# Linear attention and a gated MLP on one core: a bias preset in PSUM, decays on k, DMA transposes for seven steps, natural token order, a new order of all engines

## The chip, the core and the metric

The kernel runs on one core of a Trainium2 chip. The core has five engines that run side by side, each with its own in-order list of instructions: TensorE (PE), which multiplies matrices and transposes; VectorE (DVE); ScalarE (ACT); GpSimd (POOL); and SyncE (SP), which here only issues transfers. PE's weight loads are shown as an engine of their own, PEld. Transfers run on 16 DMA engines. They are issued from queues: SP's, ACT's, and POOL's, whose transfers also convert f32 to bf16 here. PE writes its sums into PSUM, which has eight banks of 512 f32 for each of 128 partitions; everything else lies in SBUF. The metric is the device time in microseconds; less is better.

## What is computed

Two layers in a row, for 4 sequences (batches) of 768 tokens. The first is an attention with a decay per head (8 heads of 64), in blocks of 64 tokens with a running state; the second is a gated MLP that mixes tokens by the matrix W_spatial:

```python
for b in range(nb):
    intra = np.einsum('bhic,bhjc->bhij', qb, kb) * Dmask[None]
    intra = np.einsum('bhij,bhjd->bhid', intra, vb)
    inter = np.einsum('bhid,bhde->bhie', qb * lam_pow[None], kv_state)
    out[:, :, sl] = intra + inter
    kb_dec = kb * rev_pow[None]
    kv_state = lam_block[None, :, None, None] * kv_state + np.einsum('bhsd,bhse->bhde', kb_dec, vb)
...
h = np.maximum(x @ w_in, 0.0)
u, v = (h[..., :d_ff // 2].copy(), h[..., d_ff // 2:].copy())
v_n = (v - mu) / np.sqrt(var + 1e-06)
v_s = np.einsum('ts,bsd->btd', w_spatial, v_n) + b_spatial[None, :, None]
gated = u * v_s
return (gated @ w_out).astype(np.float32)
```

The inputs q, k, v are f32, 4 x 8 x 768 x 64; w_in is 512 x 1024, w_spatial 768 x 768, w_out 512 x 512. lam, one per head, lies between 0.97 and 0.99.

## The kernel before

Each batch is cut into three steps of 256 tokens, so there are 12 steps, 0 to 11; batch 0 is steps 0 to 2. A partition holds two tokens in a row (m = 0, 1), so that a load reads 512 bytes at a time. The decay between two tokens is split into a factor of the query's position (`lq`, or its inverse form `lqn`) and one of the key's (`lv`), so the mask itself (`m01`) is only zeros and ones. In the kernel before, the key's factor is multiplied into v.

The order of all work is written out by hand in `ORDER` (lines 16 to 77). A token names an operation, its indices and, last, its engine: T is PE, D DVE, A ACT, P POOL, S SP. Each engine performs its tokens in this order, and waits where an input isn't there or a buffer isn't free; nothing overtakes. The operations of a step n are:

- LK, LQ, LV (line 184): loads of k, q, v, 512 KB each, from SP, into one of three buffers each.
- KC, QC (267): casts to bf16 into `kc`, `qc`, heads side by side in pairs. VD (292): v times the key's decay, into `vd`.
- TK, TQ (300): eight transposes on PE for each of k and q; EK, EQ (310, 313) take them out of PSUM, EQ times the query's decay. For steps 8 to 11 instead QM (277) multiplies q by the decay on the way to `qc`, and DK, DQ (283, 287) transpose by DMA, from SP's queue.
- SC (329): scores, in two halves; MK (333): the mask, from PSUM into `a_sb`; KV (345) adds to the state in a PSUM bank of its own, SS (351) copies it out; AV (366 the state's part, 375 the block's) sums the output into two banks; EX (387) copies it to `xT`, transposed as the MLP wants it.
- PV (401) and PU (439): the two halves of x @ w_in. EV and EU (406, 408) apply the ReLU; BN, RA, RD, VN (416 to 430) normalize v into `vn`.

When the three steps of a batch are done, for each of four feature groups f and two halves i of the tokens: PW (461) multiplies by W_spatial (six matmuls into one bank); GB (466, DVE) adds the bias `bsp` on the way out of PSUM into `vsb`, an f32 tile of which there are two; GM (472, POOL or DVE) multiplies by u into `gT`. Tokens within 128 are held with all even ones ahead of the odd ones in uT (and in W_spatial's columns), and GM puts them in natural order. PO (478) multiplies by w_out for each of six tiles of 128 tokens, EO (482) copies the tile to one of four `o_sb` tiles, ST (495) stores it; the last tile is copied and stored in two halves (EH, SH).

Copies go through one helper, so the profile shows them at its lines: 168 for ACT, 170 for DVE, 172 for POOL, with the tiles' names.

The weights come once, over POOL's queue: WI (239, two halves), WS (244, two halves), WO (248). A token GT (235) ahead of one of them is a copy of one element on POOL that makes POOL wait until a certain load has landed. W_spatial is transposed on PE in 72 pieces (WT, 451).

Of the kernel before, what the change touches and what calls it, by code (L numbers as in the profile page):

```python
# [8 lines left out]
FP32 = mybir.dt.float32  # L9
# [7 lines left out]
LK.0.2.S lam.A msk.P LQ.0.2.S LK.1.2.S idn.P mkc.D LV.0.2.S LB.6.T pos.P LN.6.A LK.2.2.S LL.D KC.0.2.P LX.A  # L17
LQ.1.2.S TK.0.6.T LT.0.A QC.0.2.D LQ.2.2.S TQ.0.5.T EK.0.6.A EQ.0.5.D KC.1.2.A SC.0.0.0.T LV.1.2.S SC.0.1.2.T
LT.2.A MK.0.0.0.D TK.1.6.T VD.0.2.P EK.1.6.A MK.0.1.2.D LV.2.2.S LT.1.A AV.0.0.0.T LK.3.2.S KV.0.0.T SS.0.0.A
GT.1.1.P WI.0.P QC.1.2.D KV.0.1.T AV.0.1.0.T KC.2.2.A LQ.3.2.S GT.1.1.P WI.1.P TQ.1.6.T EX.0.1.1.A TK.2.5.T  # L20
EQ.1.6.D GT.1.2.P WS.1.P EX.0.0.0.A QC.2.2.D EK.2.5.A SC.1.0.2.T LQ.4.2.S GT.1.2.P WS.0.P SC.1.1.0.T
MK.1.0.2.D TQ.2.6.T SS.0.1.A VD.1.2.P EQ.2.6.D MK.1.1.0.D SC.2.0.2.T SC.2.1.4.T MK.2.0.2.D AV.1.0.0.T KV.1.0.T
LV.3.2.S MK.2.1.4.D SS.1.0.A KV.1.1.T VD.2.2.P AV.1.1.0.T SS.1.1.A PV.0.0.6.T EX.1.1.1.A EX.1.0.0.A PV.0.1.1.T
EV.0.0.6.A AV.2.0.2.T BN.0.0.D PV.1.1.6.T EV.0.1.1.D KV.2.0.T BN.0.1.D PV.1.0.5.T SS.2.0.A EV.1.1.6.D RA.0.A
AV.2.1.2.T BN.1.1.D PU.1.0.6.T BS.S EV.1.0.5.A RD.0.D PU.0.1.4.T VN.0.0.D EX.2.1.3.A KC.3.2.P BN.1.0.D
EX.2.0.2.A PU.1.1.5.T EU.0.1.4.A EU.1.0.6.D PV.2.0.3.T RA.1.A VN.0.1.D EU.1.1.5.A RD.1.D TK.3.6.T VN.1.1.D
EV.2.0.3.A PU.2.0.2.T VN.1.0.D EK.3.6.A BN.2.0.D PV.2.1.3.T EU.2.0.2.A PU.2.1.6.T EV.2.1.3.A LK.4.2.S WT.3.2.T
BN.2.1.D EU.2.1.6.A QC.3.2.P WT.4.3.T WT.0.5.T EW.3.2.D RA.2.A WT.1.6.T LK.5.2.S EW.4.3.D EW.0.5.A WT.5.4.T
WT.2.2.T RD.2.D VN.2.1.D EW.5.4.A TQ.3.3.T QC.4.2.P VN.2.0.D PU.0.0.5.T EW.2.2.A EQ.3.3.D LQ.6.2.S EW.1.6.A
TQ.4.4.T VD.3.2.P SC.3.1.0.T EU.0.0.5.A EQ.4.4.D SC.3.0.2.T PW.0.0.1.6.T LQ.5.2.S MK.3.1.0.D PW.0.1.1.5.T  # L30
GB.0.0.1.6.D LV.4.2.S MK.3.0.2.D PW.0.1.0.4.T GM.0.0.1.P KC.4.2.A PW.0.0.0.6.T GB.0.1.1.5.D GB.0.1.0.4.D
LK.6.2.S GM.0.1.1.P TK.4.5.T GB.0.0.0.6.D PW.0.2.1.4.T GM.0.1.0.P EK.4.5.D LK.7.2.S AV.3.0.0.T GT.0.5.P WO.P
GB.0.2.1.4.D SC.4.0.2.T SC.4.1.5.T KV.3.0.T MK.4.0.2.D PW.0.3.1.4.T GM.0.2.1.P SS.3.0.A LV.6.2.S QC.6.2.P
MK.4.1.5.D KV.3.1.T AV.3.1.0.T KC.5.2.A PW.0.3.0.3.T GM.0.0.0.P SS.3.1.D GB.0.3.1.4.D LV.5.2.S QC.5.2.A
TK.5.6.T EX.3.1.1.D GM.0.3.1.P PW.0.2.0.2.T GB.0.3.0.3.D EX.3.0.0.A VD.4.2.P EK.5.6.A GM.0.3.0.D TQ.5.3.T
GB.0.2.0.2.D PV.3.1.5.T EQ.5.3.D PU.3.0.6.T EV.3.1.5.A GM.0.2.0.P AV.4.0.0.T BN.3.1.D EU.3.0.6.A SC.5.1.2.T
SC.5.0.4.T LQ.8.2.S KV.4.0.T MK.5.1.2.D PV.3.0.6.T SS.4.0.A MK.5.0.4.D KV.4.1.T EV.3.0.6.A AV.4.1.0.T LK.8.2.S
KC.6.2.P PO.0.0.3.T EX.4.0.0.A BN.3.0.D EX.4.1.1.A PO.0.1.6.T EO.0.0.3.D RA.3.A LK.9.2.S PV.4.0.2.T RD.3.D
SS.4.1.D EO.0.1.6.A VN.3.1.D VD.6.2.P VN.3.0.D PV.4.1.3.T EV.4.0.2.A ST.0.0.S TK.6.6.T BN.4.0.D EV.4.1.3.A
PO.0.2.2.T EK.6.6.A BN.4.1.D VD.5.2.P TQ.6.3.T LV.9.2.S EO.0.2.2.A PU.3.1.5.T EQ.6.3.D RA.4.A PO.0.3.6.T  # L40
# [24 lines left out]
EU.9.0.6.A AV.10.1.0.T MK.11.1.4.D PW.2.0.1.3.T EX.10.1.1.A SS.10.1.D PW.2.2.0.6.T GM.2.3.0.D GB.2.0.1.3.D
AV.11.0.4.T EX.10.0.0.D GM.2.0.1.P GB.2.2.0.6.D KV.11.0.T PV.10.0.3.T SS.11.0.D GM.2.2.0.P VN.9.0.D
# [14 lines left out]
def kernel(  # L81
# [13 lines left out]
    P = 128  # L95
# [67 lines left out]
    def bank(b, n=1):  # L163
        return ps[:, b] if n == 1 else ps[:, b:b + n]
# [89 lines left out]
    def ld_k(e, n, x):  # L254
        load(k, k_in, n, *hx(x), e)
# [279 lines left out]
```

## Time and profile before

| | |
|---|---|
| runs | 153.16, 152.09, 152.93 us; median 152.93 |
| profiled execution, first to last instruction | 151.2 us |
| bytes read from HBM, written | 24.77 MB, 6.29 MB |
| k, q and v loads, from issue to landing, median | 7.3, 7.3 and 7.1 us |
| W_spatial's two loads, from issue to landing, median | 16.1 us |
| q and k transposes by DMA, from issue to landing, median | 3.2 and 3.6 us |
| stores of 256 KB, from issue to landing, median | 2.5 us |

The profile is that of one execution. Its page lists how long each engine was busy; the span cut in 40 slices, with a digit for the busy share of each engine in tenths; the chain of work that ended last, followed back from the last instruction to what released each; and groups of equal instructions. A group reads: line, engine, operation, output<-inputs, shapes, number | busy us in all, mean ns of one | idle time of the engine just before them, and what ended most of it. The mean of a PE group holds the time through PE's pipeline, so that many in a row take less each than it says.

### The profile page before, as it was taken

Reading aid. Unit: us, or ns where it says so; the run is one execution under the profiler, and the core shown is the slowest. Engines: PE = TensorE matmul, PEld = TensorE weight load, DVE = VectorE, ACT = ScalarE, POOL = GpSimd, SP = SyncE. Lnnn points to the kernel's source line nnn. Section 1 sums busy time; section 2 is a strip of 40 time slices with the busy share of each in tenths; the row PEclk is TensorE's granted clock in tenths of the full one; section 3 lists DMA queues with packets and bytes.
Section 4 is the critical chain, followed back from the end, with each engine's and each line's share of the span. In section 5 each row is a group of like instructions: output and inputs, shape, how many; then the busy total and the mean of one; then the engine's idle time right before and its main releaser. Section 6 shows DMA issues by size and latency. Waiting matters only on the chain.

```text
span 151.2 us, 4756 instructions
## 1 busy us (share of the span) xinstructions
PE 133.6 (88%) x2026; PEld 87.2 (58%) x2026; DVE 106.9 (71%) x190; ACT 81.4 (54%) x146; POOL 75.6 (50%) x74
## 2 busy tenths in 40 slices
PE   1274947999999989977999999999999999999990
PEld 1264844677766754645766756556657655666540
DVE  1454593986999998685747799999958981936701
ACT  3987815698623837737724434765553344831161
POOL 7425980203669922780039975990293240016520
PEclk9999999999999999999999999999999999999999
DMA  3999999999988998999999799994170003121255
GB/s 108 300 290 290 283 216 216 217 248 304 281 221 237 172 301 216 269 310 342 319 341 276 142 306 311 202 208 177 41 138 4 2 4 139 57 81 72 74 219 197
DMA packets 52040, 30.73 MB, mean 203 GB/s; under 512 B 9522, under 2 KB 48946, under 8 KB 52018
## 3 DMA queue, kind: packets, MB, share of 16 engines
q1 hardware_dynamic: 49488, 27.53, 71.0%
q0 software_dynamic: 2384, 2.75, 10.6%
q8 instruction: 16, 0.26, 0.7%
q10 hardware_dynamic: 146, 0.13, 0.3%
q14 instruction: 6, 0.05, 0.1%
HBM read 24.77 MB, written 6.29 MB: 205 GB/s over the span
## 4 chain that ended last, share of the span: by engine, by line
PE 70%; DMA 16%; DVE 5%; SPq 4%; issue 2%; POOL 0%; ACT 0%; ACTq 0%
PE ps L461 20%; PE ps L439 13%; PE ps L401 13%; PE ps L478 11%; DMA q_in<-in_q_dram 10%; DMA win_sb<-in_moe_w_in_dram 6%; SPq L184 4%; PE ps L375 3%; PE ps L345 3%; PE ps L329 3%; PE ps L300 2%; PE ps L366 2%; PE ps L451 1%; DVE vsb L466 1%; DVE vn L430 1%
## 5 line engine op out<-in xcount | busy, mean ns | idle before, releaser
L472 POOL TENSOR_TENSOR gT<-vsb,uT 128x384 bf16<-128x384 f32 x27 | 30.1, 1128 | 33.6 <-DVE vsb L466 33.3
L461 PE MATMUL ps<-wt_sb,vn 128*128 128x384 bf16 x192 | 33.9, 327 | 0.0
L292 POOL TENSOR_TENSOR vd<-v_in,lv 128x1024 bf16<-128x1024 f32 x12 | 22.8, 1905 | 17.1 <-issue 6.4
L333 DVE TENSOR_TENSOR a_sb<-ps,m 128x1024 bf16<-128x1024 f32 x24 | 28.4, 1214 | 1.8 <-PE ps L329 1.6
L416 DVE BATCH_NORM_STATS2 st<-vh 128x6 f32<-128x512 bf16 x24 | 16.5, 688 | 11.9 <-ACT vh L406 11.7
L461 PEld LDWEIGHTS <-vn 128*128 128x128 bf16 x192 | 17.9, 98 | 11.9
L401 PE MATMUL ps<-win_sb,xT 128*128 128x512 bf16 x96 | 23.6, 380 | 0.8 <-DMA win_sb<-in_moe_w_in_dram 0.8
L439 PE MATMUL ps<-xT,win_sb 128*128 128x256 bf16 x192 | 24.1, 273 | 0.0
L478 PE MATMUL ps<-wout_sb,gT 128*128 128x512 bf16 x96 | 23.4, 380 | 0.0
L466 DVE TENSOR_TENSOR vsb<-ps,bsp 128x384 f32<-128x384 f32 x32 | 17.6, 552 | 6.8 <-PE ps L461 5.4
L439 PEld LDWEIGHTS <-win_sb 128*128 128x128 bf16 x192 | 18.3, 98 | 4.4
L168 ACT ACTIVATE o_sb<-ps 128x512 f32<-128x512 f32 (+1 forms) x21 | 12.3, 586 | 14.9 <-PE ps L478 10.7
L406 ACT ACTIVATE vh<-ps 128x512 bf16<-128x512 f32 x21 | 12.5, 597 | 13.6 <-PE ps L401 13.6
L406 ACT ACTIVATE uT<-ps 128x512 bf16<-128x512 f32 x22 | 13.2, 598 | 6.9 <-PE ps L439 6.7
L401 PEld LDWEIGHTS <-xT 128*128 128x128 bf16 x96 | 8.8, 98 | 9.6 <-issue 0.8
L478 PEld LDWEIGHTS <-gT 128*128 128x128 bf16 x96 | 9.0, 98 | 8.8
L168 ACT ACTIVATE s_sb<-ps 128x256 bf16<-128x256 f32 x14 | 5.3, 381 | 16.1 <-PE ps L345 16.1
L430 DVE TENSOR_SCALAR vn<-vh,mv,rstd 128x512 bf16<-128x512 bf16 x24 | 12.5, 551 | 0.3
L375 PE MATMUL ps<-a_sb,vd 64*64 64x128 bf16 x384 | 11.1, 225 | 1.7 <-DVE a_sb L333 1.0
L168 ACT ACTIVATE kc<-k_in 128x1024 bf16<-128x1024 f32 x7 | 7.4, 1056 | 8.4 <-PE ps L345 5.1
L168 ACT ACTIVATE xT<-ps 128x512 bf16<-128x512 f32 x19 | 10.5, 591 | 1.4 <-PE ps L375 1.3
L329 PE MATMUL ps<-qT,kT 64*64 64x128 bf16 x384 | 8.4, 233 | 2.5 <-DVE qT L313 2.5
(64 smaller groups left out, 155.6 us busy)
## 6 DMA issues: line engine op xcount, KB each, us to landing
k_in<-in_k_dram SPq DMA_DIRECT2D x12, 512.0 KB, 7.3
q_in<-in_q_dram SPq DMA_DIRECT2D x12, 512.0 KB, 7.3
v_in<-in_v_dram SPq DMA_DIRECT2D x12, 512.0 KB, 7.1
out_dram<-o_sb SPq DMA_DIRECT2D x23, 256.0 KB, 2.5
wsp_raw<-in_moe_w_spatial_dram POOLq DMA_DIRECT2D x2, 576.0 KB, 16.1
win_sb<-in_moe_w_in_dram POOLq DMA_DIRECT2D x2, 512.0 KB, 10.6
wout_sb<-in_moe_w_out_dram POOLq DMA_DIRECT2D x1, 512.0 KB, 10.7
bsp<-in_moe_b_spatial_dram SPq DMA_DIRECT2D x1, 384.0 KB, 8.1
```

What stands on the lines that cost most here:

```text
L168: nc.scalar.activation(out=o, in_=i, func=AF.Copy)
L292: vec(e).tensor_tensor(out=vd[n % NCA][:, h], in0=v_in[n % NIN][:, h], in1=lv[:, n % NR, h].unsqueeze(3).broadcast_to((P, h.stop - h.start ...
L333: nc.vector.tensor_tensor(out=a_sb[n % NA][:, i].rearrange("p o w j x -> p (o w) (j x)"), in0=bank(b, 2).rearrange("p o (w y) -> p (o w) y ...
L375: nc.tensor.matmul(out=po[row(w), c ^ o, c, i], lhsT=vd[n % NCA][row(c), 4 * o + u, j, :], rhs=a[row(c), i, o, w, j, :], start=(r == 0 and ...
L401: nc.tensor.matmul(out=bank(b), lhsT=x[:, c, g], rhs=win_sb[:, g, DH:DFF], start=(g == 0), stop=(g == NCH - 1))
L406: nc.scalar.activation(out=o, in_=i, func=AF.Relu)
L416: nc.vector.bn_stats(out=st6[p2][:, t], in_=vh[p2][:, t])
L439: nc.tensor.matmul(out=pu[:, f2].rearrange("p (c x) -> p c x", c=2), lhsT=win_sb[:, g, f * P:(f + 1) * P], rhs=x[:, :, g, :], start=(g == ...
L461: nc.tensor.matmul(out=bank(b)[:, 0:HW], lhsT=vn[bb % 2][:, s, f * P:(f + 1) * P], rhs=wt_sb[:, s, i * HW:(i + 1) * HW], start=(s == 0), s ...
L466: nc.vector.tensor_tensor(out=vsb[(bb * 4 + f) % NVS][:, i * HW:(i + 1) * HW], in0=bank(b)[:, 0:HW], in1=bsp[:, i * HW:(i + 1) * HW], op=A ...
L472: vec(e).tensor_tensor(out=gT[bb % 2][:, f, cols].rearrange("p (a y m) -> p a y m", m=2, y=Q64), in0=vsb[(bb * 4 + f) % NVS][:, cols].rear ...
L478: nc.tensor.matmul(out=bank(b), lhsT=gT[bb % 2][:, f, t * P:(t + 1) * P], rhs=wout_sb[:, f, :], start=(f == 0), stop=(f == NCH - 1))
```

## The change

- **Bias.** GB and `vsb` go. A new operation GP copies the bias's half (128x384, f32) into the PSUM bank (25 times on ACT, 7 on DVE); PW's six matmuls add to it, none of them starting a new sum; GM, now always on DVE, reads the bank and u and writes gT.
- **Decays.** k is multiplied by the key's factor (KM, in two halves of 128x512; 20 on POOL, 4 on DVE), which takes the place of KC; v is only cast (VC; 10 on POOL, 2 on ACT).
- **Transposes.** Steps 5 to 11 go by DMA (QM, DQ, DK); steps 0 to 4 stay on PE, those of 0 to 2 in halves.
- **Token order.** EX writes the tokens in natural order into `xT`; W_spatial is transposed in 36 whole pieces; GM has nothing to permute.
- **Tiles.** 12 output tiles for 4. The last output tile is multiplied in two halves into two banks (PH) and is no longer the last; a whole tile is stored last.
- **PSUM.** SC, MK and AV may take any two banks; SC and PU start only the first sum of a bank anew.
- **Order.** All tokens are ordered anew. Loads come nearly by step; W_in's first half is issued on POOL after `GT.0.1` and step 2's first half cast of q.

```diff
...
-LK.0.2.S lam.A msk.P LQ.0.2.S LK.1.2.S idn.P mkc.D LV.0.2.S LB.6.T pos.P LN.6.A LK.2.2.S LL.D KC.0.2.P LX.A
-LQ.1.2.S TK.0.6.T LT.0.A QC.0.2.D LQ.2.2.S TQ.0.5.T EK.0.6.A EQ.0.5.D KC.1.2.A SC.0.0.0.T LV.1.2.S SC.0.1.2.T
...
-QM.8.0.D QM.8.1.P EU.3.1.5.A ST.0.1.S RD.4.D AV.5.0.0.T VN.4.1.D EO.0.3.6.A SC.6.0.2.T VN.4.0.D SC.6.1.4.T
...
+LK.0.S lam.A msk.P mkc.D LB.0.T LN.0.A posk.P LL.D LX.A KM.0.0.D LK.1.S KM.0.1.D LQ.1.S idn.P TK.0.1.1.T
...
+EQ.0.1.0.D TQ.0.0.1.T EQ.0.0.1.D LQ.2.S QC.2.1.P GT.0.1.P WI.0.P SC.1.1.2.5.T MK.1.1.2.5.D GT.1.2.P WI.1.P
+SC.0.0.3.6.T TQ.2.1.4.T MK.0.0.3.6.D QC.2.0.A SC.0.1.0.1.T SC.1.0.2.5.T MK.0.1.0.1.D TQ.2.0.3.T MK.1.0.2.5.D
+LV.0.S VC.0.P AV.0.0.0.6.T KV.0.0.T SS.0.0.A KV.0.1.T SS.0.1.D AV.0.1.0.6.T GT.0.1.P WS.0.P LV.1.S VC.1.P
+AV.1.0.1.2.T EX.0.0.0.D EQ.2.1.4.D GT.2.1.P WS.1.P KV.1.0.T SS.1.0.A AV.1.1.1.2.T KV.1.1.T EX.1.0.1.A EX.1.1.2.A
+LK.2.S KM.2.1.P TK.2.1.5.T EK.2.1.5.D SC.2.1.0.4.T KM.2.0.P SS.1.1.D EQ.2.0.3.D TK.2.0.1.T EK.2.0.1.D EX.0.1.6.A
...
+PU.1.1.5.T BN.0.1.D RA.0.A AV.2.0.0.4.T KV.2.0.T SS.2.0.A QC.3.2.P PU.1.0.1.T LK.4.S KM.4.0.P BN.1.1.D RA.1.A
+RD.1.D VN.1.1.D LQ.4.S VN.1.0.D AV.2.1.0.4.T EX.2.1.4.D RD.0.D KM.4.1.P QC.4.2.P EX.2.0.0.A PU.0.0.6.T
+EU.0.0.6.A WO.P VN.0.0.D PV.2.0.2.T EU.1.1.5.D EU.1.0.1.A EV.2.0.2.D BN.2.0.D VN.0.1.D PV.2.1.3.T LV.3.S LQ.5.S
...
+GM.0.1.1.4.D AV.3.1.1.2.T SC.4.1.3.5.T EX.3.0.1.A QM.5.1.P DQ.5.S MK.4.1.3.5.D KV.3.1.T KM.5.0.D KM.5.1.P DK.5.S
+SC.4.0.4.6.T GP.0.2.0.1.D MK.4.0.4.6.D PW.0.0.0.0.T EX.3.1.2.A PV.3.0.3.T PU.3.0.5.T EU.3.0.5.A EV.3.0.3.A
+LV.5.S VC.5.P PW.0.2.0.1.T PV.3.1.4.T GM.0.2.0.1.D SS.3.1.A PO.0.3.6.T VC.4.A AV.4.0.2.5.T KV.4.0.T LQ.6.S
...
+AV.5.0.1.2.T KV.5.0.T LK.7.S KM.7.1.P KM.7.0.P SS.5.0.A GP.1.1.1.4.A VN.3.1.D DQ.6.S DK.6.S PV.4.0.0.T
...
+PW.3.1.0.6.T PW.3.0.0.1.T GM.3.2.1.3.D GM.3.3.1.4.D GM.3.1.0.6.D GM.3.0.1.0.D GP.3.3.0.2.D GP.3.2.0.5.A
+PW.3.2.0.5.T PH.3.5.0.3.T PH.3.5.1.4.T EH.3.5.1.4.A EH.3.5.0.3.D PO.3.3.6.T GM.3.2.0.5.D EO.3.3.6.D GM.3.0.0.1.D
+SH.3.5.0.S SH.3.5.1.S PW.3.3.0.2.T PO.3.4.0.T EO.3.4.0.A ST.3.3.S ST.3.4.S GM.3.3.0.2.D PO.3.1.4.T EO.3.1.4.A
...
-    NIN, NCA, NTR, NA, NX, NO, NVS = 3, 2, 2, 2, 3, 4, 2
+    HW = S // 2
+    NIN, NCA, NTR, NA, NX, NO = 3, 2, 2, 2, 3, 12
...
-    def split(e, n, x, src, dst):
-        copy(e, dst[n % NCA].rearrange("p u m o d -> p o (u m) d"),
-             src[n % NIN].rearrange("p (o u) m d -> p o (u m) d", o=2))
...
-    def q_m(e, n, o):
-        vec(e).tensor_tensor(out=qc[n % NCA][:, :, :, o].rearrange("p u m d -> p (u m) d"),
-                             in0=q_in[n % NIN][:, 4 * o:4 * o + 4].rearrange("p u m d -> p (u m) d"),
-                             in1=lqn[:, n % NR, 4 * o:4 * o + 4].rearrange("p u m -> p (u m)").unsqueeze(2)
-                             .broadcast_to((P, 8, D)), op=ALU.mult)
+        u = part(x)
+        copy(e, qc[n % NCA][:, u].rearrange("p u m o d -> p o (u m) d"),
+             q_in[n % NIN].rearrange("p (o u) m d -> p o u m d", o=2)[:, :, u].rearrange("p o u m d -> p o (u m) d"))
+
+    def decay(e, dst, src, ln, n, x):
+        u = part(x)
+        vec(e).tensor_tensor(
+            out=dst[n % NCA][:, u].rearrange("p u m o d -> p o (u m) d"),
+            in0=src[n % NIN].rearrange("p (o u) m d -> p o u m d", o=2)[:, :, u].rearrange("p o u m d -> p o (u m) d"),
+            in1=ln[:, n % NR].rearrange("p (o u) m -> p o u m", o=2)[:, :, u].rearrange("p o u m -> p o (u m)")
+            .unsqueeze(3).broadcast_to((P, 2, 2 * (u.stop - u.start), D)), op=ALU.mult)
+
+    def k_m(e, n, x):
+        decay(e, kc, k_in, lv, n, x)
+
+    def q_m(e, n, x):
+        decay(e, qc, q_in, lqn, n, x)
...
-    def v_d(e, n, x):
-        h = slice(*hx(x))
-        vec(e).tensor_tensor(out=vd[n % NCA][:, h], in0=v_in[n % NIN][:, h],
-                             in1=lv[:, n % NR, h].unsqueeze(3).broadcast_to((P, h.stop - h.start, 2, D)), op=ALU.mult)
+    def v_c(e, n):
+        copy(e, vb[n % NCA].rearrange("p h m d -> p (h m d)"), v_in[n % NIN].rearrange("p h m d -> p (h m d)"))
...
+    def tr(n, x, b, src):
+        u0 = part(x)
...
+    def slot(c, g):
+        return 2 * (2 * c + g % 2) + (g // 2 ^ c)
+
     def e_x(e, n, z, b):
-        xo = xT[n % NX]
-        src = bank(b).rearrange("p (c i x) -> p c i x", c=2, i=2)
-        flat = xo.rearrange("p c g x -> p (c g) x")
-        if z == 0:
-            dst = flat.rearrange("p (a i) x -> p a i x", i=2)[:, 0:4:3]
-        else:
-            dst = flat.rearrange("p (a i) x -> p a i x", i=2)[:, 1:3]
-        copy(e, dst, src)
-
+        copy(e, xT[n % NX][:, z::2].rearrange("p k (y m) -> p k m y", m=2),
+             bank(b).rearrange("p (k m y) -> p k m y", k=NCH, m=2))
...
-            for m in range(2):
-                nc.tensor.transpose(out=pw[row(m), a * P:(a + 1) * P], in_=wsp_raw[:, a, s * P + m:(s + 1) * P:2],
+            nc.tensor.transpose(out=pw[:, a * P:(a + 1) * P], in_=wsp_raw[:, a, s * P:(s + 1) * P], identity=ident)
...
+    def g_p(e, bb, f, i, b):
+        copy(e, bank(b)[:, 0:HW], bsp[:, i * HW:(i + 1) * HW])
+
     def p_w(e, bb, f, i, b):
-        HW = S // 2
         for s in range(NT):
             nc.tensor.matmul(out=bank(b)[:, 0:HW], lhsT=vn[bb % 2][:, s, f * P:(f + 1) * P],
-                             rhs=wt_sb[:, s, i * HW:(i + 1) * HW], start=(s == 0), stop=(s == NT - 1))
-
-    def g_b(e, bb, f, i, b):
-        HW = S // 2
-        nc.vector.tensor_tensor(out=vsb[(bb * 4 + f) % NVS][:, i * HW:(i + 1) * HW], in0=bank(b)[:, 0:HW],
-                                in1=bsp[:, i * HW:(i + 1) * HW], op=ALU.add)
-
-    def g_m(e, bb, f, i):
-        HW = S // 2
+                             rhs=wt_sb[:, s, i * HW:(i + 1) * HW], start=False, stop=(s == NT - 1),
+                             skip_group_check=True)
+
+    def g_m(e, bb, f, i, b):
         cols = slice(i * HW, (i + 1) * HW)
-        vec(e).tensor_tensor(out=gT[bb % 2][:, f, cols].rearrange("p (a y m) -> p a y m", m=2, y=Q64),
-                             in0=vsb[(bb * 4 + f) % NVS][:, cols].rearrange("p (a y m) -> p a y m", m=2, y=Q64),
-                             in1=uT[bb % 2][:, f, cols].rearrange("p (a m y) -> p a y m", m=2, y=Q64), op=ALU.mult)
+        nc.vector.tensor_tensor(out=gT[bb % 2][:, f, cols], in0=bank(b)[:, 0:HW], in1=uT[bb % 2][:, f, cols],
+                                op=ALU.mult)
...
-    def e_h(e, bb, t, b, x):
+    def p_h(e, bb, t, x, b):
         half = slice(x * (DM // 2), (x + 1) * (DM // 2))
-        copy(e, o_sb[(bb * NT + t) % NO][:, half], bank(b)[:, half])
+        for f in range(NCH):
+            nc.tensor.matmul(out=bank(b)[:, 0:DM // 2], lhsT=gT[bb % 2][:, f, t * P:(t + 1) * P],
+                             rhs=wout_sb[:, f, half], start=(f == 0), stop=(f == NCH - 1))
+
+    def e_h(e, bb, t, x, b):
+        half = slice(x * (DM // 2), (x + 1) * (DM // 2))
+        copy(e, o_sb[(bb * NT + t) % NO][:, half], bank(b)[:, 0:DM // 2])
...
```

## The prediction

> **What bounds the kernel now.** First the page: the engines' busy time, then the granted clock, then the DMA queues.
>
> ```profile
> PE 133.6 (88%) x2026; PEld 87.2 (58%) x2026; DVE 106.9 (71%) x190; ACT 81.4 (54%) x146; POOL 75.6 (50%) x74
> ...
> PEclk9999999999999999999999999999999999999999
> DMA  3999999999988998999999799994170003121255
> ...
> q1 hardware_dynamic: 49488, 27.53, 71.0%
> ```
>
> Two resources are full: PE, and the DMA engines (nine tenths or more in nearly every slice up to about 102 us, nearly empty after). The view by cores says clock 1.000, so no time is lost to the clock. Then the chain that ended last, in order of time (start us, us, what):
>
> ```profile
> 6.65 7.30 DMA q_in<-in_q_dram
> ...
> 14.65 9.29 DMA win_sb<-in_moe_w_in_dram
> ...
> 35.74 2.13 PE ps L451 x72
> ...
> 57.49 7.18 DMA q_in<-in_q_dram
> ...
> 64.69 0.88 DVE qc L277
> ...
> 67.67 1.14 DVE a_sb L333
> ...
> 142.33 5.19 PE ps L478 x24
> ```
>
> Up to 23.94 (14.65 + 9.29) the chain is loads, afterwards PE with one break, 57.5 to 68.85. I price PE's work by the chain's back-to-back pieces: W_spatial (L461) x6 0.97; L478 and L401 x4 0.865; L439 x8 0.875; eight transposes (L300) 0.45, so 56 ns each; L366 with L375 0.46; L345 x16 0.25; two L329 groups 0.45; W transposes 2.13 in all. Over the token list that makes 124.2 us of PE work, 7.2 of it ahead of the first L401. That piece started at 23.98, so PE was 16.8 behind pure work there. The same difference is 17.2 at the W transposes (18.4 of work, 35.7), 21.3 when step 7's K transposes start after the break (47.5 of work, 68.85), and 23.3 at PE's end (124.2 of work, 147.52). So PE lost 16.8 to the head, 4.5 between 24 and 69 (4.1 of it after the W transposes) and 2.0 in the 78 us after that. From PE's end to the span's end it is 3.7 (150.2 is the span's 151.2 less 1.0 of closing).
>
> The waits of SP's own queue and the timeline of SP matter for what is moved there:
>
> ```profile
> 79.69 2.77 SPq L287 DMA_TRANSPOSE qT<-qc  x1
> 82.56 1.87 SPq L283 DMA_TRANSPOSE kT<-kc  x1
> ```
>
> and the groups by form, for the costs:
>
> ```profile
> L472 POOL TENSOR_TENSOR gT<-vsb,uT 128x384 bf16<-128x384 f32 x27 | 30.1, 1128 | 33.6 <-DVE vsb L466 33.3 <-issue 0.2
> L292 POOL TENSOR_TENSOR vd<-v_in,lv 128x1024 bf16<-128x1024 f32 x12 | 22.8, 1905 | 17.1 <-issue 6.4 <-DMA v_in<-in_v_dram 5.8 <-PE ps L300 2.5
> L466 DVE TENSOR_TENSOR vsb<-ps,bsp 128x384 f32<-128x384 f32 x32 | 17.6, 552 | 6.8 <-PE ps L461 5.4 <-POOL gT L472 1.3
> L277 POOL TENSOR_TENSOR qc<-q_in,lqn 128x512 bf16<-128x512 f32 x6 | 7.1, 1192 | 0.0
> L277 DVE TENSOR_TENSOR qc<-q_in,lqn 128x512 bf16<-128x512 f32 x2 | 1.7, 826 | 1.4 <-DMA q_in<-in_q_dram 1.4
> ```
>
> **Part by part. PE.** Steps 5, 6 and 7 lose K and Q transposes on PE: 3 x 2 x 8 x 56 ns = 2.7 us, all on the bounding engine. W_spatial's 36 whole transposes instead of 72 half ones: 36 x 56 ns = 2.0 against 2.13, nothing. The last output tile in two halves: equal. PE's work becomes 121.5.
>
> **Bias and gate.** 32 bias adds (552 ns) leave DVE and 32 gates enter it. The gate now reads one PSUM and one SBUF operand at 128x384, the form of L466, so I take 552 ns (below: nothing faster is shown at this shape; above: the old DVE gate, 1224): zero net. The 5 old DVE gates (6.1) go, and 27 POOL gates (30.1). The preset is new: 128x384 f32 into PSUM, 7 on DVE, 25 on ACT. No row writes PSUM from either engine; the nearest are ACT 128x256 f32 (381) and 128x512 (596), so 0.49, and DVE 425 and 687, so 0.55: bounds 0.38 to 0.69, value 0.5. On ACT that is +12.2, on DVE +3.5. Each preset waits for its bank, and W_spatial's group waits for it; queued behind it on ACT are evictions, which PE waits for. PE's distance from preset to group is mostly over 2 us, so 0 to 0.3 us a piece at the tight ones. The token order moves a permutation from the gate to the copy of x into xT (pairs written two apart); the permuting DVE gates ran at 551 ns when alone, as fast as L466, so it costs nothing. Twelve output tiles end one wait of ACT for a store (2.4 in all), off the path. Decays on k lengthen the way from a k load to its transpose from one cast of 1.04 to two of 1.19, hidden where loads run ahead, and shorten that of v from 1.9 to 1.04.
>
> **The engines' sums.** DVE: gates -6.1, presets +3.5, k decay 4 x 0.83 = +3.3, casts and q decay -4.2 (5.4 to 1.2), K evictions +2.1, Q evictions of two steps fewer -1.9, output and ReLU and x evictions taken over from ACT +2.0 +3.4 +2.6 +1.4, rest -0.3: 106.9 becomes about 112.7. ACT: +12.2, casts of v +2.1, K evictions -6.0, casts of k and q -7.9, evictions given to DVE -8.4: 81.4 to 73.4. POOL: gates, decay of v, casts and q decay -67.3; 33 half decays at 1.19, 10 casts of v at 1.04, q casts 4.2 are +53.9: 75.6 to 62.2. PE stays the fullest engine, but DVE has 112.7 in a span that I expect at 145, 78% for 71%.
>
> **Head.** Loads land every 1.8 us: the first at 4.9 (the timeline's POOL cast starts at 4.97), the sixth at 13.95. W_in's first half is issued behind the sixth load now (14.65), in the change behind the fifth (12.15) and its half cast of q (0.53): about 13.0. Its 9.3 us give 22.3. PE then has 7.0 of work behind it (step 2's first K half waits on POOL past both W_spatial issues, about 20.3, still earlier): 15.4 behind instead of 16.8, a gain of 1.4. The W issues stay a queue of about 3.7 us each, so the W transposes gain the same.
>
> **The break at 57 to 69.** DVE stands at step 8's q decay until that load lands (57.49 + 7.18), and the norms and masks behind it hold PE. The change's load order is by step, so this goes: -4.1. Late next is the decay of half of step 5's k, which the change puts on DVE: its load is the eighth behind W_in, due at 44 to 45, and DVE reaches it at about 47, but W_out's issue now falls at about 40. In the trace a load issued next to W_out (45.25) landed at 57.6, some 5 us later than the load rate says. Behind the waiting decay stand a preset and step 4's masks, and PE waits for both. 0 to 4, I take 1.5, as the load is due ahead of what W_out delays.
>
> **Steps 5 to 11 by DMA.** 14 transposes stand in SP's in-order queue, 8 before; SP holds each until decays are done, with loads behind it. At step 5 SP waits from about 42 until the decays end at 48 to 50, with two or three loads in flight. In the trace the last pair, on an otherwise idle queue, was issued at 108.40 and 110.18 and the second landed 3.1 after its issue; I read 1.5 us of all DMA engines each. Six more: 9 us of DMA time, in a stage where the loads run ahead: the last k load was issued at 84.49 and its cast ran at 108.26, so the cover is about 15 us, less the 6 us by which PE is to be earlier. Step by step the pairs arrive 0 to 2 us from when PE wants them. Bounds 0 to 8 for steps 6 to 11, value 1.0. [...]
>
> **DVE's coupling.** From step 5's first mask to step 5's norms DVE has 11.2 us of work against 11.9 of PE; before W_spatial of batch 2 it has 11.4 against 11.9; before that of batch 3 the last norm is ready 0.3 late. +1.2, from 0 to 7 (24 normalizations at 0.41 alone but up to 1.1 beside POOL in the timeline). [...]
>
> **Tail.** The last store is whole (its copy 0.6 for 0.4, landing 2.0 for 1.7), +0.3 with a short wait for the last gate.
>
> **The sum.** PE -2.7, head -1.4, break -4.1, the old late losses -2.0 (replaced by those named); added 1.5 + 1.0 + 1.2 + 0.3 = 4.0. Net -6.2: span 151.2 to 145.0. The runs' median is 152.9, 1.7 above the profiled span; I add that: **146.7**.
>
> **Rivals.** (1) *SP's queue becomes the bound: slower.* Transposes hold the loads behind them; the queue stands 6 to 8 us at step 5, 2 to 3 at each of steps 6, 7 and 8, plus 9 us of DMA time, about 24 in all. Against: most of it falls where loads are already queued. For: DMA is full until 102 us now. Cover is about 9 to 15; it decides for slower once more than 17 us are lost. 24 less 15 is 9 more: 146.7 + 8 to 9 = 155. (2) *DVE becomes the bound.* Each stage's DVE work at the contended durations adds about 0.3 x 24, less the 1.2 counted: 152.5, about no change. For: DVE idles only 1.8 us in all ahead of its 24 masks (L333's group). Against: the waits show 11.7 us of DVE idle for ReLU outputs. (3) *The edits do nothing for the pace*, since the loads set it and their bytes don't fall: break and head stay, 146.7 + 5.5 = 152.2.
>
> **Chances.** The forecast 0.60, better than 142.7 (all added waits nothing) 0.06, rival 1 0.17, rivals 2 and 3 together 0.17. A measurement here tells about 1% from no change: 151.4 to 154.5. Rivals 2 and 3 split: 0.06 faster, 0.11 same. Faster 0.72, same 0.11, slower 0.17. The range goes from 142.5 (no added wait) to 154.5, short of rival 1.
>
> **What would show it.** PE busy near 130, DVE near 113, POOL near 62. First L401 near 22.3; no DVE wait for a q load at 57 to 69; step 5's SC starting at about 53 to 55 and step 9's at 98 to 101. Wrong if: PE idles over 1 us ahead of L329 with the releaser a transposed qT or kT (rival 1); DVE over 80% with PE idle behind norms and masks (rival 2); first L401 later than 24 or DVE idle for k_in at 45 to 52 (W_out's effect, or rival 3).

## The result, and the profile after

| | before | after |
|---|---|---|
| median of the runs | 152.51 us (152.05 to 153.16, 4 runs) | 173.66 us (172.02 to 175.13, 4 runs) |
| profiled execution: time, span | 152.9, 151.2 us | 173.52, 171.7 us |

The ratio is 1.136, with a 95% interval from 1.128 to 1.144: 14% slower, where 146.7 us were forecast. Ratios here leave disturbed runs out and medians don't, so the two can differ by a per cent.

The page of the changed kernel: busy time, slices, the chain by engine and by line, then groups.

```profile
PE 139.0 (81%) x1946; PEld 86.9 (51%) x1946; DVE 113.3 (66%) x209; ACT 74.9 (44%) x148; POOL 56.3 (33%) x70
...
PE   1295879699997991999856994999789968999991
...
PEclk9999999999999999699999998799999999999999
DMA  4999999999932799999900699999992740360045
...
PE 60%; DVE 24%; ACT 10%; issue 3%; POOL 1%; DVEq 0%; POOLq 0%
PE ps L467 17%; PE ps L478 12%; DVE a_sb L342 10%; PE ps L406 10%; PE ps L444 6%; DVE vn L435 4%; PE ps L384 3%; DVE st L421 3%; PE ps L337 3%; PE ps L306 3%; ACT lq L218 3%; PE ps L354 3%; PE ps L375 2%; DVE gT L473 1%; ACT xT L171 1%
...
L473 DVE TENSOR_TENSOR gT<-ps,uT 128x384 bf16<-128x384 f32 x32 | 16.9, 551 | 8.5 <-PE ps L467 8.1
L171 ACT ACTIVATE xT<-ps 128x512 bf16<-128x512 f32 x17 | 11.7, 742 | 8.0 <-PE ps L384 5.0
```

DMA, full until 102 us before, now has holes, so loads are not what is short. DVE is busy for a smaller share than before (66% for 71%), yet holds 24% of the chain, and its mask L342, to whose reading of PSUM the forecast gave no term, holds 10%. A busy share can't show that; the waits do. TensorE's waits, longest first (line waited at, its releaser: us in all, times, longest):

```profile
PE ps L337 <- DVE a_sb L342: 7.6, 6, 1.6
PE ps L478 <- DVE a_sb L342: 6.1, 2, 3.8
...
PE ps L467 <- DVE a_sb L342: 1.8, 1, 1.8
PE ps L406 <- DVE a_sb L342: 1.7, 1, 1.7
```

That is 17.2 us behind the masks. In the kernel before it was 2.7:

```profile
PE ps L300 <- DVE a_sb L333: 1.2, 1, 1.2
PE ps L375 <- DVE a_sb L333: 1.0, 1, 1.0
PE ps L366 <- DVE a_sb L333: 0.5, 1, 0.5
```

And in the changed kernel L478, L467 and L406 multiply by W_out, W_spatial and W_in: they read nothing that the mask writes. The longest of these waits, in the timeline (start us, us, engine, line; in brackets the engine's idle time before it and what ended that):

```profile
64.76 0.75 ACT L171 ACTIVATE xT<-ps 128x512 bf16<-128x512 f32 x1
...
65.54 2.36 DVE L342 TENSOR_TENSOR a_sb<-ps,m 128x1024 bf16<-128x1024 f32 x2 [2.75 <-ACT xT L171]
...
67.96 1.31 PE L478 MATMUL ps<-wout_sb,gT 128*128 128x512 bf16 x4 [3.83 <-DVE a_sb L342]
```

By the token order the two masks are MK.5.1.1.4 (banks 1 and 4) and MK.5.0.0.6 (banks 0 and 6), the copy on ACT is EX.4.0.2 (bank 2) and the product is PO.0.5.3 (bank 3). DVE waits 2.75 us for a reader of bank 2, and TensorE 3.83 for masks that leave bank 3 alone. Both banks lie *between* those that a mask reads. In the kernel before every mask reads two neighbours; here 18 of 24 pairs lie apart, and the one instruction reads them with a stride, `ps[:, b0:b1 + 1:b1 - b0]`. By the profile, each of these waits is for a semaphore of the program. Why these should cover the banks between, the trace does not say; whether they do is what theory A below puts to the test.

### The profile page after: what moved, and what is told of

Its sections match the earlier page's. It is cut to its first block, busy times and chain, and to the rows that moved or that the text cites. A ratio compares the mean times of both kernels' runs of the same rounds, so it can differ in the third digit from the quotient of the medians.

```text
span 171.7 us, 4582 instructions
## 1 busy us (share of the span) xinstructions
PE 139.0 (81%) x1946; PEld 86.9 (51%) x1946; DVE 113.3 (66%) x209; ACT 74.9 (44%) x148; POOL 56.3 (33%) x70
## 3 DMA queue, kind: packets, MB, share of 16 engines
q0 software_dynamic: 2384, 2.75, 9.4%
## 4 chain that ended last, share of the span: by engine, by line
PE 60%; DVE 24%; ACT 10%; issue 3%; POOL 1%; DVEq 0%; POOLq 0%
PE ps L467 17%; PE ps L478 12%; DVE a_sb L342 10%; PE ps L406 10%; PE ps L444 6%; DVE vn L435 4%; PE ps L384 3%; DVE st L421 3%; PE ps L337 3%; PE ps L306 3%; ACT lq L218 3%; PE ps L354 3%; PE ps L375 2%; DVE gT L473 1%; ACT xT L171 1%
## 5 line engine op out<-in xcount | busy, mean ns | idle before, releaser
L467 PE MATMUL ps<-wt_sb,vn 128*128 128x384 bf16 x192 | 34.3, 326 | 3.1 <-DVE a_sb L342 1.8
L342 DVE TENSOR_TENSOR a_sb<-ps,m 128x1024 bf16<-128x1024 f32 x24 | 29.1, 1218 | 8.0 <-PE ps L337 3.4
L276 POOL TENSOR_TENSOR kc<-k_in,lv 128x512 bf16<-128x512 f32 x20 | 20.5, 1041 | 37.6 <-PE ps L354 19.5
L478 PE MATMUL ps<-wout_sb,gT 128*128 128x512 bf16 x92 | 24.6, 404 | 6.1 <-DVE a_sb L342 6.1
L406 PE MATMUL ps<-win_sb,xT 128*128 128x512 bf16 x96 | 25.1, 400 | 2.4 <-DVE a_sb L342 1.7
L467 PEld LDWEIGHTS <-vn 128*128 128x128 bf16 x192 | 17.9, 98 | 15.7 <-issue 2.3
L473 DVE TENSOR_TENSOR gT<-ps,uT 128x384 bf16<-128x384 f32 x32 | 16.9, 551 | 8.5 <-PE ps L467 8.1
L171 ACT ACTIVATE o_sb<-ps 128x512 f32<-128x512 f32 (+1 forms) x18 | 10.4, 583 | 25.2 <-PE ps L478 20.0
L276 POOL TENSOR_TENSOR qc<-q_in,lqn 128x512 bf16<-128x512 f32 x13 | 13.4, 1048 | 16.6 <-DMA q_in<-in_q_dram 8.0
L171 ACT ACTIVATE ps<-bsp 128x384 f32<-128x384 f32 x25 | 11.9, 491 | 13.5 <-DVE a_sb L342 8.1
L337 PE MATMUL ps<-qT,kT 64*64 64x128 bf16 x384 | 11.2, 238 | 8.1 <-DVE a_sb L342 7.6
L478 PEld LDWEIGHTS <-gT 128*128 128x128 bf16 x92 | 8.9, 101 | 15.5 <-DVE a_sb L342 4.0
L406 PEld LDWEIGHTS <-xT 128*128 128x128 bf16 x96 | 9.3, 103 | 14.1 <-issue 4.2
L175 POOL CAST vb<-v_in 128x1024 bf16<-128x1024 f32 x10 | 10.4, 1050 | 16.7 <-DMA v_in<-in_v_dram 7.4
L411 ACT ACTIVATE vh<-ps 128x512 bf16<-128x512 f32 x17 | 10.0, 595 | 12.4 <-DVE a_sb L342 6.3
L337 PEld LDWEIGHTS <-kT 64*64 64x64 bf16 x384 | 7.7, 116 | 12.3 <-issue 10.9
## 6 DMA issues: line engine op xcount, KB each, us to landing
win_sb<-in_moe_w_in_dram POOLq DMA_DIRECT2D x2, 512.0 KB, 11.6
```

Of the source, the lines that this page charges most:

```text
L171: nc.scalar.activation(out=o, in_=i, func=AF.Copy)
L175: nc.gpsimd.tensor_copy(out=o, in_=i)
L276: vec(e).tensor_tensor(out=dst[n % NCA][:, u].rearrange("p u m o d -> p o (u m) d"), in0=src[n % NIN].rearrange("p (o u) m d -> p o u m d" ...
L337: nc.tensor.matmul(out=pa[o][row(c), w, j], lhsT=kT[n % NTR][row(o), u, j, c * Q64:(c + 1) * Q64], rhs=qv(n, o, u, c), start=(w == 0 and j ...
L342: nc.vector.tensor_tensor(out=a_sb[n % NA][:, i].rearrange("p o w j x -> p o w (j x)"), in0=ps[:, b0:b1 + 1:b1 - b0].rearrange("p o (w y) ...
L406: nc.tensor.matmul(out=bank(b), lhsT=x[:, slot(c, g)], rhs=win_sb[:, g, DH:DFF], start=(g == 0), stop=(g == NCH - 1))
```

## The experiments

Theories: **A**, the mask holds every bank from b0 to b1; **B**, DVE is the bound and masks come late; **C**, transposing DMAs and SP's queue set the pace; **E**, presets hold banks too long; later **F**, TensorE's rate, which in the head is about half (eight transposes of the kernel before took 1.03 us at 10.4 us and 0.62 at 18.5); **G**, TensorE's own code arrives late (the DMA page of the changed kernel has a queue named "instruction", q8, with 15 packets and 0.25 MB); **H**, GpSimd slows DVE's norms. Line numbers shift by a few in the variants.

### The baseline

All variants have plain DMAs of the same bytes for the transposing ones, so from step 5 on (step 8 in the kernel before) they compute something else.

```diff
-nc.sync.dma_start_transpose(kT..., kc...)
+for h in (slice(0, 2), slice(2, 4)):
+    nc.sync.dma_start(out=kT[:, h]..., in_=kc[:, h]...)
```

> Baseline of the experiments. Edit: each transposing DMA of the changed kernel (L289, L293) becomes two plain DMAs of the same bytes from kc to kT and from qc to qT, in the same place of SP's order; the transposition of steps 5 to 11 is left out, so what these steps compute is another thing, while every instruction of the engines, every order and every wait stays. Theory A (the mask of L342 holds every bank from b0 to b1): 171 to 175 us, as the changed kernel. Theory C (transposing DMAs and SP's queue behind them set the pace): SP is freed of some of 14 issues of 1.2 to 3.5 us, and the time falls to 160 or below.

Measured: 173.35 us, ratio 1.129 [1.120, 1.139]. The stand-in is the changed kernel in time, and C falls for it: how these 14 transfers are done costs nothing there that can be measured (173.66 us with transposing ones), and no wait of TensorE in the changed kernel has a DMA as releaser.

### The mask's banks

```diff
-in0=ps[:, b0:b1 + 1:b1 - b0]...           (one instruction)
+for o, b in ((0, b0), (1, b1)):
+    in0=bank(b)..., out=a_sb[:, i, o]...  (standin_by_bank)
+for w in range(2):
+    in0=ps[:, b0:b1 + 1:b1 - b0, w * 256:(w + 1) * 256]...  (standin_halves)
```

> Edit on the stand-in: the masking of step SC's products (L342), one instruction over the two banks b0 and b1, becomes two instructions of one bank each; order, banks and all else stay. Theory A: the waits of TensorE behind L342 that are not for its own bank go (PV.0.1 1.9 us, SC.4.0 1.2, PO.0.5 4.1, PW.1.1.0 1.6, PW.1.0.0 2.0, SC.7.1 1.7, PO.1.0 2.4, SC.9.1 1.7, PO.2.1 2.0: 18.6 us in all), 24 more DVE instructions give some back: 155 to 159 us. Theory B (DVE is the bound: the mask comes late because DVE is loaded): 173 to 177 us, since DVE only gets more instructions. Theory C: no change from the stand-in.

> Control of the run before, on the stand-in: the mask of L342 is again two instructions, but each over both banks (one half of the columns each), so that the span from b0 to b1 stays. Theory A: the waits stay and DVE has 24 more fixed costs: 173 to 178 us. If merely smaller instructions are what helps (a shorter hold of DVE, earlier start of AV), it falls like the run before, to 155 to 160.

Measured: 155.55 us by bank (ratio to the kernel before 1.008 [1.002, 1.014]), 174.26 in halves (a single run). Both have equally many instructions on DVE, and some 18 us lie between them. In halves the waits stay:

```profile
PE ps L339 <- DVE a_sb L345: 8.0, 6, 1.6
PE ps L481 <- DVE a_sb L345: 6.1, 2, 4.0
```

That speaks for A, and not for B. TensorE's waits of standin_by_bank begin with

```profile
PE ps L308 <- DVE kc L276: 3.4, 1, 3.4
PE ps L201 <- DVE one_row L235: 2.9, 1, 2.9
PE ps L357 <- issue: 1.7, 1, 1.7
PE ps L459 <- DVE wt_sb L173: 1.6, 1, 1.6
```

and the mask, the releaser of four of the groups in the changed kernel, is none of its releasers. Now the same thing done to the kernel before, whose order, engines and work stay:

```diff
+R = (0, 3, 1, 4, 2, 5, 6, 7)
-return ps[:, b]...
+return ps[:, R[b]]
...
+in0=ps[:, b0:b1 + 1:b1 - b0]...   (the mask; b0, b1 = R[b], R[b + 1])
```

> The kernel before with its eight PSUM banks renamed (logical 0..7 lie in physical 0,3,1,4,2,5,6,7), so that its pairs (0,1), (2,3), (4,5) lie at 0 and 3, 1 and 4, 2 and 5, and its mask reads them as a strided pair as in the changed kernel; its 8 transposing DMAs are two plain DMAs of the same bytes each, so the transposition of four steps is left out. Order, engines and work of the engines are as before. Theory A: the mask now holds two more banks and the same kind of waits comes up: 160 to 175 us. Theories B and C, and any theory by which a bank's place does not matter: 151 to 154 us.

> The kernel before with its banks renamed as in before_apart, and its mask in two instructions of one bank each (its transposing DMAs again replaced by plain ones). Theory A: the waits of before_apart (163.3 us) go, and what is left over the kernel before is the price of 24 more DVE instructions: 152 to 156 us. If the renaming costs for another reason (where in PSUM a bank lies, engines that disturb each other on neighbouring banks), it stays at 160 to 165.

Measured: 163.31 us renamed (a single run), 151.74 renamed with the mask by bank (ratio 1.005 [0.998, 1.012]). Its waits when renamed:

```profile
PE ps L466 <- DVE a_sb L338: 4.0, 4, 1.3
ACT xT L170 <- DVE a_sb L338: 3.8, 2, 2.5
...
PE ps L333 <- DVE a_sb L338: 2.6, 1, 2.6
```

So where a bank lies costs nothing that can be measured, a strided read over others' banks 11.6 us, and 24 instructions more on DVE nothing that can be measured. A is shown from both sides.

### What is left at 155.5

Runs of one kernel spread by 2 to 5 us here (153.01 to 156.90 for standin_by_bank), so differences of 1 to 2 us between the variants below are read from waits and durations in the traces, and the medians alone don't show them. Three single edits on standin_by_bank come first. The presets, with the bias left out:

> On the stand-in with its mask by bank (155.6 us): the 32 presets of the bias (L463) are left out, and the first product of each group starts its bank; the spatial bias is missing from what is computed. Prices what the presets cost where they stand. The prediction took 0.5 us each and had them beside PE's work: then 154.5 to 155.6. If the products of W_spatial wait for presets (theory E, banks held longer by a preset ahead of the products): 151 to 154.

Rows written whole into xT, with the natural token order left out:

> On the stand-in with its mask by bank: the copy of attention's output into xT (L400) writes whole rows in place of every second column, as the kernel before did; the natural token order is left out. The strided copies took 742 (ACT) and 724 ns (DVE) against 591 and 681 before, 24 of them, so at most 3 us of engine time goes. If that engine time is beside PE's work: 154.8 to 155.6; if first products with W_in wait for it, 152 to 154.

And three copies of W_spatial moved from DVE to ACT (`EW.0`, `EW.4`, `EW.1`, ahead of `RA.2`):

> On the stand-in with its mask by bank: three copies of transposed W_spatial out of PSUM (EW of 0, 4, 1) go from DVE to ACT and ahead of step 2's norms. In the trace of standin_by_bank PE waits 1.77 us at WT.3 (41.7 us) for a bank that EW.0 on DVE frees only at 41.1, behind five norm instructions, while ACT has nothing to do from 37.6 to 40.7. If DVE's queue (theory B, now at this one place) sets that wait: 153.5 to 154.5 us, and WT.3 starts before 40.5. If the products of W_spatial wait for the norms anyway: no change.

Measured: 155.60, 155.01 and 156.03 us. Presets and token order are hidden, as forecast; E falls. The third did what it should, with no wait left at WT.3 (1.6 us in standin_by_bank), and the time did not follow: a miss. The gain was lost at stops of another kind, which add up to 2.9 us in standin_by_bank and to 4.5 in this run. The longest in standin_by_bank:

```profile
63.34 0.23 PE L357 MATMUL ps<-vb,kc 64*64 64x64 bf16 x4
65.31 0.38 PE L357 MATMUL ps<-vb,kc 64*64 64x64 bf16 x12 [1.75 <-issue]
65.62 1.74 PE L409 MATMUL ps<-win_sb,xT 128*128 128x512 bf16 x4
```

TensorE stops in the middle of 16 alike products, for nothing the profile names. Counting all its instructions in the trace (matmuls, weight loads and a few waits), 1729 have begun when it stops; at the other such stops it is 449 and 2241. All three are 193 past a multiple of 256. One of the two DMA queues named "instruction" (q8) moves packets of 16 KB, 15 in this run, about one for each 256 of TensorE's 3909 instructions (16 KB over 256 makes 64 bytes an instruction). Their times, from the trace's packets (us):

```
run               block begun     packet for the next   next block begun   stop
standin_by_bank   1473 at 58.73   62.84 to 64.04        1729 at 65.31      1.75
early_loads       1473 at 57.21   58.41 to 59.53        1729 at 64.33      none
code_shift        1729 at 58.78   62.71 to 63.90        1985 at 68.36      none
```

G, as these times suggest it: a packet leaves about when the block before it is begun, in early_loads 1.2 us after, but up to 4.3 us after in by_bank_wt_on_act, where by the theory more loads are ahead of it; its instructions run 1.3 us after it has landed at the earliest. From block 1473 of standin_by_bank, 256 short ones (KV, AV, SC) were through in 4.6 us. Two tests, both on by_bank_wt_on_act: SP's order, and 64 tiny products of zeros in the head that move every later instruction by 128 places.

> On by_bank_wt_on_act (156.0 us), SP's order alone: the loads LV.5, LQ.6, LK.6, LQ.7 and LK.7 go ahead of DQ.5, where SP stands idle from 42.0 to 51.6 us; nothing else is moved. Theory G (TensorE's own instructions come in packets of 16 KB, 256 instructions; the packet is asked for as the packet before begins to be used and lands behind the loads in flight; where 256 short matmuls are through sooner, TensorE stands): in by_bank_wt_on_act the packet for the instructions from number 1729 was asked for at 58.4, began to land at 62.1 and TensorE stood from 63.2 to 64.6, and after it the granted clock was 0.5 to about 70. With fewer loads in flight at 58 to 63 that packet starts within 1.5 us, the stop at KV.5.0 and the low clock behind it go, 3 to 4 us together: 152 to 153.5 us. If the stop is something else (a wait for vb or kc that the profile does not name): the stop stays, 155.5 to 156.5.

> On by_bank_wt_on_act: 64 tiny matmuls of zeros (128 instructions with their weight loads) are put on TensorE behind LB, in the 3.4 us in which it waits for the first k, and their results are not used; every later instruction of TensorE stands 128 places further on, nothing else is moved. Theory G: the stops, which stood at number 449, 1729 and 2241 (each 193 past a multiple of 256), stay at those numbers and so move to other work: the 1729th is then 128 instructions earlier in the program, in SC.5.1 and PO.0.3 and not in KV.5.0; with more time since the packet before, or less, the stop changes its size, and the one at KV.5.0 is gone. Otherwise the stop stays in KV.5.0 at what is now number 1857. In time: 152 to 157 us, as the stops fall; if TensorE is also granted the full clock sooner by the work in the head, the head is up to 1.5 us shorter.

Measured: 156.92 and 154.42 us. In early_loads the stop at 1729 is gone (1.4 us at 449 stay), but step 5's kT, now behind five loads, keeps TensorE 2.4 us (`PE ps L277 <- DMA kT<-kc`): a miss in time, by a new wait. The low clock that its expectation puts behind the stop was not there to be gained: in the profile of by_bank_wt_on_act the granted clock is 1.00 throughout from 60 to 72 us, while it is 0.50 from 66 to 68 in standin_by_bank. In code_shift no such stop over 0.3 us is left anywhere, and the median falls by 1.6 us. Not all of that need be the stops: the tiny products also keep TensorE at work in the head, where the half rate ends at 25.3 us in place of 29.1. The boundaries are shown; what the chip does between packet and first instruction is not. Single crossings took up to 2.0 us (by_bank_plain_x).

From code_shift on: a product moved into a gap (`PO.0.4` behind `PU.4.0`), and the decays of steps 6 and 7 left out.

> On code_shift (154.4 us): one output product, PO.0.4, is moved on TensorE from ahead of PV.5.0 to behind PU.4.0, into the gap of 1.36 us in which TensorE waits for step 5's norms (71.42 to 72.59 in code_shift). If that gap is a chain PV.5, its statistics, its norms, then the products of W_spatial, it starts 0.87 us sooner and the gap is filled: 153.2 to 153.9 us. If something that does not depend on PV.5 sets it: no change.

> On code_shift (154.4 us): GpSimd's multiplications of q and k by the decays for steps 6 and 7 (8 instructions of about 1.05 us, between 60 and 73 us) are left out, so these steps compute with older data; nothing else is moved. In code_shift a norm on DVE (vn, 128x512 bf16) takes 0.40 us with GpSimd idle (10 of them) and 0.90 beside it (11). Theory H (GpSimd's instruction slows DVE's norms, and TensorE waits for the norms): the five norms between 62.3 and 72.5 take 0.40 each and not 0.66 to 1.13, the wait at PW.1.1.0 (1.36 us) shrinks below 0.5, and the time falls by 1 to 2.5 us, to 152 to 153.4. If the norms are slow for another reason (data, position): they stay at 0.66 to 1.13, and the time moves by under 0.5.

Measured: 153.99 and 152.66 us. The gap is 1.18 us by the profile (the expectation has 1.36) and shrinks to 0.42. For the norms, three in a row on DVE, code_shift first (GpSimd runs kc, L220, from 70.30 to 72.39), then no_decay_6_7:

```profile
70.45 2.41 DVE L382 TENSOR_SCALAR vn<-vh,mv,rstd 128x512 bf16<-128x512 bf16 x3
```

```profile
69.74 1.06 DVE L382 TENSOR_SCALAR vn<-vh,mv,rstd 128x512 bf16<-128x512 bf16 x3
```

H holds for the norms: 0.41 us each without GpSimd, while in code_shift the two beside it take 1.04 and 1.13 and the third, when it has ended, 0.41. TensorE's wait for them there is gone. Leaving work out can also help by itself, so the decays were put back, behind the norms; that took place on top of two runs on TensorE's rate. For these, products of zeros fill TensorE's waits at 15.5 to 20 us (keep_busy), and those at 3.5 to 6.9 too (warm_head).

> On fill_gap (154.0 us): 8 products of zeros (128x512, results not used) are put on TensorE where it waits between 15.5 and 20.1 us, into banks that are free there; they take 1.7 us at the full rate. [...] If the head is set by its chain of loads, masks and the arrival of W_in alone: 154 or a little more, as the products of zeros only add work.

> On keep_busy: four of the larger products of zeros ahead of the tiny ones in the head (3.5 to 6.9 us, where TensorE waits for the first k) and one behind the first transposes, so that TensorE comes warm to its first work. Theory F: transposes of half a step take 0.3 and not 0.61 us from 7 us on, and the first masks start up to 1.5 us sooner, but q's arrival at 10.5 us holds the second half of the head: 0 to 1 us less than keep_busy. If the rate in the head does not matter: the same as keep_busy.

Measured: 154.83 and 152.40 us. The first product with W_in, in fill_gap and in warm_head:

```profile
23.19 1.89 PE L353 MATMUL ps<-win_sb,xT 128*128 128x512 bf16 x4
```

```profile
23.56 1.03 PE L357 MATMUL ps<-win_sb,xT 128*128 128x512 bf16 x4
```

Four alike products, at 1.89 and 1.03 us. keep_busy was to bring the full rate sooner, and did, without a gain in time (154.83 us, fill_gap 153.99): TensorE was at it from 16.7 to 22 us (AV.1.1 0.53 for 0.85), came sooner to number 705, another 193 past a multiple of 256, stood 1.7 us for its packet, and fell back to the half rate until 30. warm_head stands there 1.5 us too, but keeps the rate, and its median is 1.6 us below that of fill_gap. In keep_busy F and G work on each other.

> On warm_head (152.4 us): GpSimd's decays for steps 6 and 7 (the 8 instructions that no_decay_6_7 left out) are done, but held back by a copy of one element that waits for the norms: those of step 6 begin behind step 3's norms, those of k of step 7 behind step 5's; the transposing stand-in DK.7 and LK.8 change places in SP's order. Theory H (norms on DVE take 0.9 to 1.1 us beside a GpSimd instruction and 0.40 alone): the five norms between 62 and 72 us take 0.40 to 0.66, TensorE's waits of 0.8, 0.7 and 0.6 us at PU.4.1, PU.5.1 and PW.1.1.0 shrink to under 0.8 in all: 150.7 to 151.8 us, faster than the kernel before by 1%. If q and k of steps 6 and 7 then come too late for their products (SC.6 at 75.4): a wait of 0.5 to 2 us there, 152.4 to 154.

> On decay_later (156.8 us), GpSimd's order alone: the two decays of q for step 8 go behind those of k for step 7. In decay_later GpSimd stood 5.6 us at the former, for a q that landed at 76, so k of step 7 was done at 80.1 and SC.7 waited 2.8 us; the norms before took 0.41 us, and TensorE's waits of 0.6 to 0.8 us at PU.4.1, PU.5.1 and PW.1.1.0 were gone. Theory H with that order as the cause of decay_later's loss: k of step 7 is done near 73.7, SC.7 does not wait, 150.7 to 152.2 us, at or below the kernel before. If the norms' gain is taken back by later waits anyway: 153 to 155.

Measured: 156.81 us for decay_later, a miss: five of the six norms between 63 and 72 us took 0.41, but GpSimd stood 5.6 us at a decay of step 8 ahead of step 7's, and SC.7 waited 2.7. With these two exchanged, decay_order has 152.60 us (149.32 to 154.74), the kernel before 152.94 beside it. That is no lower than warm_head's 152.40, so what faster norms are worth in time is not shown. The ratio to the kernel before, 0.984 [0.973, 0.994], rests on its two fastest runs of six; by the medians of all runs it is 0.998. All of the changed kernel's engine work and bytes are in it, with plain DMAs for transposing ones. So the change with these repairs is level with the kernel before, and faster is not shown; with transposing DMAs this was not run.

## Why the prediction was wrong

**The step that failed is one that was left out.** The forecast's own list of the change had "SC, MK and AV may take any two banks", and its working has no term for it. It counted what an instruction costs and who is queued behind it, not which banks it holds. Measured, that is 17.8 us (173.35 less 155.55) of the 27 us by which the forecast missed. The other 9 us are below. Neither the range nor a rival had it: the sum of "DVE's coupling", 0 to 7, is about DVE's load, and DVE was idle while the masks waited (8.0 us ahead of L342, 1.8 ahead of L333 before). What TensorE lost at these waits was followed by more: in the changed kernel the granted clock is 0.65 and 0.50 in the two stretches of 2 us from 68 to 72 us, after the 3.83 us wait, and 0.53 and 0.61 from 106 to 110, after one of 2.22. Step 5's SC started at 62.9 and not at 53 to 55, step 9's at 123.0 and not at 98 to 101.

The rest, against standin_by_bank, where that step is repaired:

- **PE.** The count fell as said (1946 matmuls for 2026). Busy was 139.0, not 130: the 96 products with W_in, alike in both kernels, were busy for 25.1 us (23.6 before), as some ran at the half rate. So busy time here does not measure work alone.
- **Bias, gate, token order.** Gates 551 ns (552 foreseen), presets 491 and 549 (500). The token order was put at nothing, read from gates of DVE; ACT's copies into xT do cost more, 742 for 591, but beside other work: leaving out presets or token order moved the median by 0.5 us or less.
- **Engines.** DVE 113.3 (112.7), ACT 74.9 (73.4), POOL 56.3 (62.2; its half decays took 1.04 us and not 1.19): near, and no help, since no sum of an engine's work shows a wait.
- **Head, -1.4: wrong sign.** L406 (first L401 before) started at 25.86, not 22.3. W_in's first half took 10.3 us and not 9.3 from its issue and landed at 23.50, which alone takes 1.2 us, most of the gain, away; masks' banks and the half rate did the rest. With the mask by bank it started at 24.33, and TensorE was at the half rate until 28.3. The forecast had read a clock of 1.000 and "no time is lost to the clock". In the head of the kernel before, eight transposes took 1.03 us at 6 to 11 us and 0.61 at 68.85: that head ran at about the half rate too, and the pieces' prices, from stretches at the full rate, were used for it.
- **Break, -4.1: gone and filled again.** DVE's wait for step 8's q is gone, and k of step 5 landed at 45.5, so the 1.5 for W_out was not needed. But standin_by_bank loses 1.6 us at WT.3 (41.7 us) and, where the break was, about 3.5 between 63 and 70: 1.75 at the code block and, an estimate from granted clocks of 0.95, 0.50 and 0.69 in the stretches of 2 us from 64 to 70, 1.7 to the low rate behind it.
- **DMA transposes, +1.0.** No wait of TensorE in the changed kernel has a DMA of qT or kT as releaser: 0, hidden. The cover is thin: early_loads, with plain DMAs, shows 2.4 us once they queue behind loads.
- **DVE's coupling, +1.2.** The forecast saw norms at 0.41 and up to 1.1 and priced only DVE's own queue; the norms beside GpSimd were worth at most 1.8 us (code_shift less no_decay_6_7, which also leaves the work out). The five decays on DVE took about 0.70 us each (0.83 foreseen).
- **Rivals.** None. SP's queue (1) had the right direction, slower, for a wrong reason: what was to show it, TensorE waiting ahead of L337 (L329 before), did appear, 7.6 us, but with the mask as releaser. "First L401 later than 24" was named as a sign of failure and was one, for causes that the forecast did not list.

## What to carry to other kernels

Before letting a buffer lie anywhere, look at what each instruction's access *spans*, since its waits can cover all between its first and its last bank: two instructions of one bank each cost nothing measurable here, one with a stride cost 18 us. Where a wait's releaser writes nothing that the waiting line reads, look at the places that both touch. And when the bounding engine is to run tighter, price what slack had hidden: its clock after a gap (0.50 here after a wait of 3.83 us), its code blocks (stops of up to 2.0 us), and how its neighbours slow each other (norms at 0.41 us alone, up to 1.23 beside GpSimd).

## What the runs showed of the hardware

- TensorE's stops without a releaser began at its instructions number 449, 1729 and 2241 (standin_by_bank) and 705 (keep_busy), each 193 past a multiple of 256, and q8 moved about one packet of 16 KB for each 256 instructions. The stops took up to 2.0 us (by_bank_plain_x); in standin_by_bank 256 short instructions were through in 4.6 us, faster than the next packet came. With 64 tiny products ahead of them no such stop over 0.3 us was left (code_shift).
- TensorE started at about half rate in these runs and fell back after some waits: four transposes took 0.61 us at 7 and still at 25.5 us in the changed kernel, 0.40 from 9 us on in warm_head. The clock's view shows 1.00 there, so the durations tell it, not the view. The two low stretches in the changed kernel (granted clock 0.50 from 68.6 to 72.0 us and from 106.1 to 109.5) lose about 1.7 us each, an estimate from the granted clocks above. How long a wait it takes was not shown: standin_by_bank fell back at 66 us after a wait of only 1.75, and warm_head kept the full rate through one of 1.5.
- A norm that reads one SBUF tile in bf16 took 0.38 to 0.41 us on DVE alone and mostly 0.57 to 1.23 beside a GpSimd instruction (the kernel before and the changed one, 24 norms each); three of the changed kernel that shared at most 0.18 us with one still took 0.41.
